# Hash attention and router: groups of four units, the mask's bits on four row quarters, first pair by tokens

## The chip, the cores and the metric

The kernel runs on one core of one Trainium2 chip. The metric is the time of one execution on the device in microseconds; of several executions the median is given. Lower is better.

## What is computed

The reference is attention with a hash mask, then a router with eight experts. B = 4 batches, 8 heads, S = 768 tokens, D = 64; the router sees N = 3072 tokens of 512 features.

```python
q_bits = (einsum('bhsd,dk->bhsk', q, proj) > 0)      # 6 bits for every query and key
k_bits = (einsum('bhsd,dk->bhsk', k, proj) > 0)
mask = bucket(q_bits)[:, :, :, None] == bucket(k_bits)[:, :, None, :]
scores = where(mask, q @ k.T / sqrt(D), -1e9)
attn = softmax(scores) @ v                            # per head
x = attn of all heads side by side                    # 3072 x 512
e = argmax(cosine(x, expert_emb) / tau); gate = softmax prob of e
out = gate * (relu(x @ w1[e]) @ w2[e])                # 512 -> 1024 -> 512
```

## The kernel before

**Tiling of the attention.** Two heads of a batch are a pair; there are 16 pairs (`pairs`), 4 to a batch. Features lie on partitions: head 0 on rows 0 to 63, head 1 on rows 64 to 127. A unit (`units`) is one block of 128 keys (c of 6) against one half of the queries (s of 2, 384 each) for both heads: 12 units in a pair, 192 in all. `scores(u)` (L553) issues for a unit two f32 matmuls, K = 64, one per head on its half of the array's rows (L560), and two bf16 matmuls that add the mask's bits into the same PSUM banks (L563): equal bits leave the score, unequal ones pull it far down. The exponential (L566, ScalarE) then writes the tile p, and VectorE adds p into `acc` (L570, L573), from which the row sums come. `attend(u)` (L579) multiplies p with the values (L585), both heads on a column half of the array each, K = 128. An f32 matmul is two passes in the trace; a bf16 matmul one.

**Order.** The loop at L720 goes over groups of G = 3 units; g counts the groups of a pair (0 to 3). In each turn it issues the scores of a group, then `attend` for the group before, and after them by hand a step of the pair's other work. `in_order` (L430) ties all instructions of an engine to this order. The steps, with g: sums of the pair before (`sums`, L596: row sums by TensorE L602, ScalarE copy, DMAs za and zc on SP) at 0; transposes of the next pair's q and k by VectorE (`prep_features`, L512) at 0 and 1; squares for the router's norm (`add_squares` ScalarE at 0, `added_squares` VectorE L424 at 1); `scale` (L612: reciprocal L615, DMA zd out, DMA rz back in broadcast) at 1, with the load of the pair three ahead (`load`, `load_values`), a piece of expert weights, the router's logits (L192) in every fourth pair, and `square` (L519: ScalarE, L524, with accumulator read) of the next pair; bits of the next pair (`prep_bits`, L529) at 2 and `store` (L629); `scaled` (L623: multiplication with rz) at 3. `run(n)` advances the placing of tokens in expert lists (`place`, VectorE), of which the last batch's share sits in pair 14, with `fill` (L323), `lists`, `places` (L338) and the first gathers by GpSimd (`fetch`, L379).

**Bits.** `prep_bits` multiplies `proj2` with the features of a pair in eight matmuls (64 rows x 32 columns, L538) into one PSUM tile, ScalarE copies it as bf16 to `hs` (L541), and eight VectorE operations (L545 for q, L549 for k) compare with 0 and write 6 and 12 rows to `qb` and `kb`, which hold 64 rows for each head.

**Buffers.** `banks()` (L448) hands out three PSUM tiles of two banks in rotation; scores, sums, bits and logits all take the next one. Six tiles p (`pts`, 2 G), two `av` banks.

**Start.** `load(0)` (L492) brings q and k of pair 0 in 128-byte pieces on the SP and ScalarE queues, 28 matmuls of ones (WARM) keep TensorE busy, GpSimd's queue brings `proj2`, VectorE transposes q and k (L517).

After the attention the experts run (L937 on), untouched by the diff.

Of the kernel before, what the change touches and what calls it, by code (L numbers as in the profile page):

```python
# [26 lines left out]
def kernel(  # L27
# [104 lines left out]
    nc.vector.scalar_tensor_tensor(out=qcon[:], in0=ksub[:], scalar=2.0 * BIT, in1=qcon[:], op0=ALU.mult, op1=ALU.add)  # L132
# [25 lines left out]
    nc.gpsimd.dma_start(gd[ZC:N, :].rearrange("(p c) o -> p (c o)", c=NC), zrow[:, 0:NC])  # L158
    nc.gpsimd.dma_start(gd[N : N + 1, :], zrow[0:1, NC : NC + 1])
    nc.gpsimd.dma_start(xd[ZC * NQ : (ZC + 1) * NQ, :].rearrange("i (f j) -> (i f) j", j=4), zrow[:, 0:4])  # L160

    proj2 = const.tile([P, 2, 32], F32, name="proj2")
    nc.vector.memset(proj2[:], 0.0)
    for h in range(2):
        nc.gpsimd.dma_start(proj2[h * D : (h + 1) * D, h, 0:HB].rearrange("d (r n) -> d r n", r=2),
                            proj.unsqueeze(1).broadcast_to([D, 2, NB]))
# [260 lines left out]
    units = [(pr, s, c) for pr in range(len(pairs)) for s in range(2) for c in range(NC)]  # L427
# [10 lines left out]
    with ExitStack() as at:  # L438
# [9 lines left out]
        def banks():  # L448
            return ps_w.tile([P, 2, 512], F32, name="banks", tag="banks")


        WARM = 28
        G = 3
# [6 lines left out]

        qbs = [ep.tile([P, 2, SH], BF16, name=f"qb{i}") for i in range(2)]
        kbs = [ep.tile([P, 2, SH], BF16, name=f"kb{i}") for i in range(2)]
        for t in qbs:
            nc.gpsimd.tensor_copy(out=t[:], in_=qcon[:, 0:1].unsqueeze(2).broadcast_to([P, 2, SH]))
        for t in kbs:
            nc.gpsimd.memset(t[:], 0.0)
# [24 lines left out]
        ld, feat, acc, av, zcs, rzs = {}, {}, {}, {}, {}, {}  # L491
        def load(pr):  # L492
            if pr >= len(pairs):
                return
            b, j = pairs[pr]
            qk = ldp.tile([P, 2, S // 32, 32], F32, name="qk", tag="qk")
            vt = ldp.tile([P, 2, NC, D], F32, name="vt", tag="vt", bufs=4)
            for g in range(NQ):
                for i, src in enumerate((q, k)):
                    (nc.scalar if pr < 2 and i else nc.sync).dma_start(  # L500
                        qk[32 * g : 32 * (g + 1), i].rearrange("t (c a) f -> t c a f", c=NC),
                        src[b, 2 * j + g // 2].rearrange("(a t c) d -> t c a d", t=32, c=NC)[
                            :, :, :, 32 * (g % 2) : 32 * (g % 2 + 1)])
            ld[pr] = (qk, vt)
# [7 lines left out]
        def prep_features(pr, i):  # L512
            if pr >= len(pairs):
                return
            t = augp.tile([P, 2, SH], F32, name="qt" if i == 0 else "kt", tag="qt" if i == 0 else "kt")
            feat[pr, i] = t
            nc.vector.transpose(t[:].rearrange("p s n -> p (s n)"), ld[pr][0][:, i].rearrange("p n f -> p (n f)"))  # L517
# [11 lines left out]
        def prep_bits(pr):  # L529
            if pr >= len(pairs):  # L530
                return
            b = (qbs[pr % 2], kbs[pr % 2])
            ps = banks()
            for i in range(2):
                for s in range(2):
                    for h in range(2):
                        r0 = 32 * (2 * i + s)
                        nc.tensor.matmul(ps[r0 : r0 + 32, h, 0:SH], lhsT=proj2[h * D : (h + 1) * D, h, :],  # L538
                                         rhs=feat[pr, i][h * D : (h + 1) * D, s, :], start=True, stop=True)
            hs = rp.tile([P, 2, SH], BF16, name="hs", tag="hs", bufs=1)  # L540
            nc.scalar.copy(out=hs[:], in_=ps[:, :, 0:SH])  # L541
            for s in range(2):
                for h in range(2):
                    r0 = 32 * s
                    nc.vector.tensor_scalar(out=b[0][h * D : h * D + NB, s], in0=hs[r0 : r0 + NB, h], scalar1=0.0,  # L545
                                            scalar2=2.0 * BIT, op0=ALU.is_gt, op1=ALU.mult)
                for h in range(2):
                    r0 = 64 + 32 * s
                    nc.vector.tensor_scalar(out=b[1][h * D : h * D + HB, s], in0=hs[r0 : r0 + HB, h], scalar1=0.0,  # L549
                                            scalar2=ksub[r0 : r0 + HB, 0:1], op0=ALU.is_gt, op1=ALU.subtract)  # L550


        def scores(u):  # L553
            pr, s, c = units[u]
            qt, kt, qb, kb = feat[pr, 0], feat[pr, 1], qbs[pr % 2], kbs[pr % 2]
            ps = banks()
            kc = slice((c % HC) * P, (c % HC + 1) * P)
            rows = [slice(h * D, (h + 1) * D) for h in range(2)]
            for h in range(2):
                nc.tensor.matmul(ps[:, h, 0:SH], lhsT=kt[rows[h], c // HC, kc], rhs=qt[rows[h], s, :],  # L560
                                 start=True, stop=False)
            for h in range(2):
                nc.tensor.matmul(ps[:, h, 0:SH], lhsT=kb[rows[h], c // HC, kc], rhs=qb[rows[h], s, :],  # L563
                                 start=False, stop=True)
            p = pts[u % NPT]
            nc.scalar.activation(p[:, :, 0:SH], ps[:, :, 0:SH], ACT.Exp, scale=ESCALE)  # L566
            if c == 1:
                a = op.tile([P, 2, SH], F32, name="acc", tag="acc", bufs=3)
                acc[pr, s] = a
                nc.vector.tensor_tensor(out=a[:], in0=pts[(u - 1) % NPT][:, :, 0:SH], in1=p[:, :, 0:SH], op=ALU.add)  # L570
            elif c > 1:
                a = acc[pr, s]
                nc.vector.tensor_tensor(out=a[:], in0=a[:], in1=p[:, :, 0:SH], op=ALU.add)  # L573
# [5 lines left out]
        def attend(u):  # L579
            pr, s, c = units[u]  # L580
# [3 lines left out]
            for h in range(2):  # L584
                nc.tensor.matmul(ps[h * D : (h + 1) * D, 0 : SH + 1], lhsT=vt[:, h, c, :], rhs=p[:, h, 0 : SH + 1],  # L585
                                 start=(c == 0), stop=(c == NC - 1))
# [118 lines left out]
        load(0)  # L705

# [3 lines left out]
        nc.sync.dma_start(emb[:], expert_emb[:, :])  # L710
        nc.sync.dma_start(tau_t[:], tau.unsqueeze(0).broadcast_to([E, 1]))
# [4 lines left out]
        for pr in range(1, 3):  # L716
            load(pr)
            load_values(pr)
        U, PU = len(units), 2 * NC
        for u0 in range(0, U + G, G):  # L720
# [3 lines left out]
            run(7 if j == 2 and end else 3)  # L724
            for u in range(u0, u0 + G):
                if u < U:
                    scores(u)
                if end and j == 2:
                    if g == 1 and u == u0 + 1:
                        begin(b, spare(2 * E * NC))  # L730
                    elif g == 2:
                        run(2 if u < u0 + 2 else 99)
                    elif g == 3 and u == u0 + 1:
                        fill(b, spare(4 * NS))
                        listed = lists(slots, src[0][:], NS, rp)
            if u0 == U:
                scaled_last(len(pairs) - 1, 0)
            for u in range(u0 - G, u0):
                if 0 <= u < U:
                    attend(u)  # L740
                if u0 == U and u == U - G:
                    scale_last(len(pairs) - 1, 1)
            if end and j == 2 and g == 3:
                places(listed, pos[0][:], NS, banks()[:, 0], rp)
                early = [fetch(pos[0], 0, 2, ZC + 1)]
            if pr == len(pairs):
                break
            if g == 0:
                if pr > 0:
                    sums(pr - 1)  # L750
                prep_features(pr + 1, 0)
                if pr > 1:
                    add_squares(pr - 2, rp)
                if pr == 2:
                    prep_experts(1)
                if j == 2 and b >= 0:
                    gates(b, rp, 0)
            elif g == 1:
                prep_features(pr + 1, 1)
                if pr > 1:  # L760
                    added_squares(pr - 2)
# [19 lines left out]
            elif g == 2:  # L781
                prep_bits(pr + 1)
                if pr > 1 and not (end and j == 2):
                    store(pr - 2)
                if j == 2 and b >= 0 and not end:
                    gates(b, rp, 2)
                if j == 3 and end:
                    bound(1)
            else:
                if pr > 0:  # L790
                    scaled(pr - 1)
                if pr == 1:
                    prep_experts(0)
# [4 lines left out]
                if j == 2 and end:  # L798
                    store(pr - 2)
                    gates(b, rp, 2)  # L800
# [3 lines left out]
                if j == 3 and end:  # L804
                    scale_last(pr, 0)
# [562 lines left out]
```

## Time and profile before

| | |
|---|---|
| median of 3 runs | 720.61 us (719.82 to 723.15) |
| profiled execution, its own time | 721.9 us |
| its span | 719.9 us |
| mean granted TensorE clock | 0.991 |
| TensorE matmul busy | 691.8 us, 96% of the span |
| VectorE busy | 479.4 us |
| ScalarE busy | 307.5 us |
| GpSimd busy | 193.9 us |

Busy times by stage, from the trace (us; the second row is the attention's steady part, the fourth the experts):

| stretch | PE | DVE | ACT | POOL |
|---|---|---|---|---|
| 0 to 9.8 | 7.97 | 5.27 | 1.49 | 9.12 |
| 9.8 to 336.2 | 320.69 | 261.77 | 221.26 | 7.59 |
| 336.2 to 360 | 21.89 | 16.87 | 11.82 | 18.45 |
| 360 to 719.9 | 341.21 | 195.49 | 72.91 | 158.77 |

How to read the profile: PE is TensorE's matmuls, PEld its weight loads, DVE VectorE, ACT ScalarE, POOL GpSimd, SP the engine that issues most DMAs. The ends of matmuls are modelled, so starts are what to compare. A form such as 64*128 after an operation is its rows * columns of the array. In the groups of instructions a row ends with the busy time, the mean of one, and the idle time of the engine ahead of it with what ended it. A wait for several things is put down to the last. A profiled execution is one run; its time lies 1.3 us above the median.

### The profile page before, as it was taken

What the parts mean: (1) busy time and instruction counts of PE and PEld (TensorE: products, weight loads), DVE (VectorE), ACT (ScalarE), POOL (GpSimd) and SP (SyncE); (2) the same over time, 40 slices, a digit from 0 to 9 for tenths busy, and PEclk for the clock granted to TensorE, in tenths of its full rate; (3) what the DMA queues carried; (4) which work ended last, traced back from release to release, by engine and by line L of the source; (5) the groups of instructions that cost most, each with busy time, mean ns of one, the idle gap of its engine ahead of it and who ended that gap; (6) DMA issues with size and microseconds to landing.
All of it is one profiled execution on the core that took longest, in us unless ns stands there. A gap on an engine that the chain in (4) does not pass through costs nothing.

```text
span 719.9 us, 11583 instructions
## 1 busy us (share of the span) xinstructions
PE 691.8 (96%) x4197; PEld 427.7 (59%) x4197; DVE 479.4 (67%) x984; ACT 307.5 (43%) x565; POOL 193.9 (27%) x202
## 2 busy tenths in 40 slices
PE   8999999999999999998899998999999999999992
PEld 6444443444434444343475666969797879797970
DVE  5867787789778897698752022798867786866100
ACT  2777765767757767665420111213222222222210
POOL 5000000000000000003714763246554647350160
PEclk9999999999999999999999999999999999999997
DMA  9733477743678645523581139335454545443320
GB/s 141 125 54 75 74 112 140 135 78 93 118 141 140 127 70 118 92 34 64 98 264 37 56 132 321 129 139 183 143 170 141 167 149 172 146 157 132 123 75 20
DMA packets 198337, 87.90 MB, mean 122 GB/s; under 512 B 171569, under 2 KB 179565, under 8 KB 198264
## 3 DMA queue, kind: packets, MB, share of 16 engines
q1 hardware_dynamic: 183704, 68.35, 40.5%
q0 software_dynamic: 6720, 13.67, 6.3%
q10 hardware_dynamic: 7840, 4.98, 2.5%
q8 instruction: 37, 0.61, 0.4%
q14 instruction: 36, 0.29, 0.2%
HBM read 82.57 MB, written 13.31 MB: 133 GB/s over the span
## 4 chain that ended last, share of the span: by engine, by line
PE 79%; DVE 7%; POOL 4%; issue 3%; DMA 3%; ACT 1%; SPq 0%; POOLq 0%; DVEq 0%; ACTq 0%
PE ps_h L1091 15%; PE banks L560 15%; PE av L585 15%; PE ps_y L984 11%; PE ps_h L1120 10%; PE ps_h L976 6%; PE banks L563 4%; POOL xg L379 3%; DVE acc L573 2%; PE banks L538 2%; PE banks L602 1%; DMA proj<-in_proj_dram 1%; DVE kt L517 1%; DMA out_dram<-y,osrc 0%; DMA qk<-in_k_dram 0%
## 5 line engine op out<-in xcount | busy, mean ns | idle before, releaser
L566 ACT ACTIVATE p<-banks 128x768 f32<-128x768 f32 x192 | 152.1, 812 | 44.8 <-PE banks L563 42.0
L560 PE MATMUL banks<-qt,kt 64*128 64x384 f32 x768 | 162.3, 500 | 0.0
L585 PE MATMUL av<-p,vt 128*64 128x385 f32 x768 | 138.5, 495 | 0.0
L573 DVE TENSOR_TENSOR acc<-acc,p 128x768 f32<-128x768 f32 x128 | 122.1, 954 | 20.7 <-ACT p L566 11.0
L379 POOL DMA_INDIRECT xg<-xd,pos x96 | 103.6, 1079 | 101.3 <-ACT ht L1095 41.1
L1066 DVE TENSOR_TENSOR tm<-ps_h,tm 128x192 f32<-128x192 f32 (+1 forms) x210 | 72.2, 368 | 56.5 <-PE ps_h L1120 30.4
L560 PEld LDWEIGHTS banks<-qt,kt 64*128 64x128 f32 x768 | 64.8, 186 | 60.9 <-issue 32.7
L984 PE MATMUL ps_y<-w,ht 128*128 128x512 f32 x224 | 98.4, 593 | 0.0
L585 PEld LDWEIGHTS av<-p,vt 128*64 128x64 f32 x768 | 49.4, 136 | 75.8 <-issue 73.8
L229 POOL TENSOR_TENSOR nrm<-l,half 128x6 f32<-128x6 f32 x4 | 5.4, 1340 | 264.6 <-DVE l L206 264.6
L984 PEld LDWEIGHTS ps_y<-w,ht 128*128 128x128 f32 x224 | 41.9, 190 | 47.4 <-issue 47.1
L563 PE MATMUL banks<-qb,kb 64*128 64x384 bf16 x384 | 63.7, 323 | 1.1 <-DVE kb L549 1.1
L1095 ACT ACTIVATE ht<-tm 128x192 f32<-128x192 f32 x96 | 32.6, 362 | 74.7 <-DVE tm L1066 74.7
L1091 PE MATMUL ps_h<-tx,xT 128*128 128x192 f32 x288 | 56.0, 332 | 2.6 <-DVE xT L1026 2.6
L991 DVE TENSOR_SCALAR y<-ps_y,gg 128x512 f32<-128x512 f32 x8 | 6.0, 751 | 70.7 <-PE ps_y L984 70.7
L1091 PEld LDWEIGHTS ps_h<-tx,xT 128*128 128x128 f32 x288 | 49.3, 194 | 2.9 <-DVE xT L1026 2.9
L995 POOL DMA_INDIRECT out_dram<-y,src x24 | 28.2, 1175 | 79.8 <-ACT y L1111 17.2
L978 ACT ACTIVATE ht<-ps_h 128x128 f32<-128x128 f32 (+1 forms) x48 | 15.0, 313 | 74.9 <-PE ps_h L976 73.3
L976 PE MATMUL ps_h<-xge,w 128*128 128x256 f32 (+1 forms) x256 | 43.2, 328 | 0.7 <-DVE xT L663 0.7
L976 PEld LDWEIGHTS ps_h<-xge,w 128*128 128x128 f32 x256 | 38.6, 191 | 5.8 <-issue 1.7
L1091 PE MATMUL ps_h<-xgt,w 128*128 128x192 f32 x192 | 39.5, 328 | 0.0
L570 DVE TENSOR_TENSOR acc<-p,p 128x768 f32<-128x768 f32 x32 | 30.5, 954 | 11.9 <-ACT p L566 11.8
(274 smaller groups left out, 845.4 us busy)
## 6 DMA issues: line engine op xcount, KB each, us to landing
w<-in_moe_w_dram SPq DMA_DIRECT2D x20, 2048.0 KB
qk<-in_q_dram SPq DMA_DIRECT2D x64, 96.0 KB
vt<-in_v_dram SPq DMA_DIRECT2D x16, 384.0 KB
xd<-xb SPq DMA_DIRECT2D x64, 96.0 KB
rz<-zd SPq DMA_DIRECT2D x30, 192.0 KB
qk<-in_k_dram SPq DMA_DIRECT2D x56, 96.0 KB
w<-in_moe_w_dram SPq DMA_DIRECT2D x8, 512.0 KB
w<-in_moe_w_dram ACTq DMA_DIRECT2D x2, 2048.0 KB
```

Source lines behind the costliest of these rows:

```text
L379: dma = nc.gpsimd.indirect_dma_start(out=xg[:, g, :], out_offset=None, in_=xd[0 : width * NQ, :], in_offset=bass.IndirectOffsetOnAxis(ap=p ...
L560: nc.tensor.matmul(ps[:, h, 0:SH], lhsT=kt[rows[h], c // HC, kc], rhs=qt[rows[h], s, :], start=True, stop=False)
L563: nc.tensor.matmul(ps[:, h, 0:SH], lhsT=kb[rows[h], c // HC, kc], rhs=qb[rows[h], s, :], start=False, stop=True)
L566: nc.scalar.activation(p[:, :, 0:SH], ps[:, :, 0:SH], ACT.Exp, scale=ESCALE)
L573: nc.vector.tensor_tensor(out=a[:], in0=a[:], in1=p[:, :, 0:SH], op=ALU.add)
L585: nc.tensor.matmul(ps[h * D : (h + 1) * D, 0 : SH + 1], lhsT=vt[:, h, c, :], rhs=p[:, h, 0 : SH + 1], start=(c == 0), stop=(c == NC - 1))
L976: nc.tensor.matmul(ph[:, 0:n], lhsT=w1s[i][:, d, f * P : (f + 1) * P], rhs=xt[:, d, 0:n], start=(d == 0), stop=(d == ND - 1))
L984: nc.tensor.matmul(py[:], lhsT=ht[:, f, j * P : (j + 1) * P], rhs=w2s[i][:, f, :], start=(f == 0), stop=(f == NF - 1))
L1066: nc.vector.tensor_tensor(out=out, in0=ps, in1=s, op=ALU.add)
L1091: nc.tensor.matmul(out, lhsT=l[:, d, f * P : (f + 1) * P], rhs=r[:, d, :], start=(d == 0), stop=(d == ND // 2 - 1))
L1095: acted[0] = nc.scalar.activation(ht[:, f + j * NF // 2, k * HT : (k + 1) * HT], c, ACT.Relu).ins
L1120: nc.tensor.matmul(out, lhsT=l[:, f, :], rhs=r[:, f, :], start=(f == 0), stop=(f == NF // 2 - 1))
```

## The change

G becomes 4, so a pair of heads has three groups (g of 0 to 2), p has eight tiles, and the steps are dealt to the groups anew. The key blocks of a pair are taken alternately from the two halves of the keys; `scores` now issues two units at once: scores of the first on their half rows, four bit matmuls of 32 rows (two heads, two key blocks, one row quarter each, into four banks), scores of the second. To that end `qb` holds the query bits on both quarters of a head, in the two orders, and `kb` one key half on each quarter; the constants ride in the compare (`qthr`, `qmul`). Pair 0 is loaded by tokens, in 256-byte pieces, turned by TensorE and copied by ScalarE (q) and VectorE (k). `proj2` comes on SP's queue, pair 1 is loaded earlier, WARM is 14.

```diff
-        WARM = 28
-        G = 3
+        WARM = 14
+        G = 4
...
-    units = [(pr, s, c) for pr in range(len(pairs)) for s in range(2) for c in range(NC)]
+    units = [(pr, s, c, c // 2 + c % 2 * HC) for pr in range(len(pairs)) for s in range(2) for c in range(NC)]
...
+            if pr == 0:
+                for i, src in enumerate((q, k)):
+                    for h in range(2):
+                        (nc.scalar if i else nc.sync).dma_start(by_token(qk, i)[:, :, h * D : (h + 1) * D],
+                                                                src[b, h].rearrange("(p c) d -> p c d", c=NC))
+                return
...
+            if pr == 0:
+                ps = banks()
+                for c in range(NC):
+                    nc.tensor.transpose(ps[:, c // HC, c % HC * P : (c % HC + 1) * P], by_token(ld[pr][0], i)[:, c, :], ident[:])
+                (nc.vector.tensor_copy if i else nc.scalar.copy)(out=t[:], in_=ps[:, :, 0:SH])
+                return
...
+            for h in range(2):
+                for i, o, n in ((0, 0, 32 + HB), (32, 0, HB), (0, 32, HB)):
+                    nc.vector.tensor_scalar(out=b[0][h * D + o : h * D + o + n, int(n == HB)], in0=hs[i : i + n, h],
+                                            scalar1=qthr[i : i + n, 0:1], scalar2=qmul[i : i + n, 0:1],
+                                            op0=ALU.is_gt, op1=ALU.mult)
+            for h in range(2):
+                n = slice(64, 64 + 32 + HB)
+                nc.vector.tensor_scalar(out=b[1][h * D : h * D + 32 + HB], in0=hs[n, h], scalar1=0.0,
+                                        scalar2=ksub[n, 0:1], op0=ALU.is_gt, op1=ALU.subtract)
...
+        def scores(u):
+            pr, s, _, c = units[u]
+            qt, kt, qb, kb = feat[pr, 0], feat[pr, 1], qbs[pr % 2], kbs[pr % 2]
+            ps = [banks() for _ in range(2)]
+            kc = slice(c * P, (c + 1) * P)
+            def score(i):
                 for h in range(2):
+                    n = slice(h * D, (h + 1) * D)
+                    nc.tensor.matmul(ps[i][:, h, 0:SH], lhsT=kt[n, i, kc], rhs=qt[n, s, :], start=(i == 0), stop=(i == 1))
+            score(0)
             for h in range(2):
+                for i in range(2):
+                    n = slice(h * D + 32 * i, h * D + 32 * (i + 1))
+                    nc.tensor.matmul(ps[i][:, h, 0:SH], lhsT=kb[n, kc], rhs=qb[n, s ^ i, :], start=(i == 1), stop=(i == 0))
+            score(1)
...
+        for h in range(2):
+            nc.sync.dma_start(proj2[h * D : (h + 1) * D, h, 0:HB].rearrange("d (r n) -> d r n", r=2),
+                              proj.unsqueeze(1).broadcast_to([D, 2, NB]))
...
+        load(1)
         load_values(0)
...
+            if g == 1 and 1 < pr < len(pairs):
+                added_squares(pr - 2)
+            run(7 if g == 1 and j == 2 and end else 4)
...
             if g == 0:
                 if pr > 0:
                     sums(pr - 1)
-                prep_features(pr + 1, 0)
+                    for i in range(2):
+                        prep_features(pr + 1, i)
...
+                if j == 2 and end:
+                    begin(b, spare(2 * E * NC))
...
             elif g == 1:
-                prep_features(pr + 1, 1)
-                if pr > 1:
-                    added_squares(pr - 2)
+                if pr == 0:
+                    for i in range(2):
+                        prep_features(pr + 1, i)
+                prep_bits(pr + 1)
                 if pr > 0:
                     scale(pr - 1)
                 load(pr + 3)
...
-            elif g == 2:
-                prep_bits(pr + 1)
-                if pr > 1 and not (end and j == 2):
-                    store(pr - 2)
...
             else:
+                if j == 2 and end:
+                    places(listed, pos[0][:], NS, banks()[:, 0], rp)
+                    early = [fetch(pos[0], 0, 2, ZC + 1)]
                 if pr > 0:
                     scaled(pr - 1)
+                if pr > 1:
+                    store(pr - 2)
```

The steps after `load(pr + 3)` in g = 1 stay where they were: logits, then `square(0)` and `square(pr + 1)`, then `gates` (L241).

## The prediction, on record before the result

> **What bounds the kernel now.** I read the head of the page and its chain first, then TensorE's table of waits, then the timeline of a few groups, last ScalarE's part of it.
>
> ```profile
> span 719.9 us, 11583 instructions
> ...
> PE 79%; DVE 7%; POOL 4%; issue 3%; DMA 3%; ACT 1%; SPq 0%; POOLq 0%; DVEq 0%; ACTq 0%
> ...
> L566 ACT ACTIVATE p<-banks 128x768 f32<-128x768 f32 x192 | 152.1, 812 | 44.8 <-PE banks L563 42.0
> ```
>
> TensorE holds 79% of the chain that ended last. ScalarE's exponentials (L566) wait for TensorE, not the other way round. The table of waits for 9 to 336 us shows that the attention stage is nearly pure matmul:
>
> ```profile
> engine line waited for: us in total, times, longest us
> PE banks L192 <- DVE ssq__163 L424: 2.5, 3, 1.0
> PE banks L338 <- DVE half__3160 L330: 1.2, 1, 1.2
> PE banks L563 <- DVE kb L549: 1.1, 1, 1.1
> PE av L323 <- DVE col L316: 0.8, 1, 0.8
> ```
>
> So what TensorE does per group of units sets the time there, and the first row (router logits waiting for a sum of squares) is the largest wait left. One group of three units, from the timeline (start, duration):
>
> ```profile
> 152.44 0.92 PE L560 MATMUL banks<-qt,kt 64*128 64x384 f32 x4
> 153.19 0.33 PE L563 MATMUL banks<-qb,kb 64*128 64x384 bf16 x2
> 153.35 0.81 PE L560 MATMUL banks<-qt,kt 64*128 64x384 f32 x4
> 153.99 0.33 PE L563 MATMUL banks<-qb,kb 64*128 64x384 bf16 x2
> 154.16 0.81 PE L560 MATMUL banks<-qt,kt 64*128 64x384 f32 x4
> 154.80 0.33 PE L563 MATMUL banks<-qb,kb 64*128 64x384 bf16 x2
> 155.06 2.16 PE L585 MATMUL av<-p,vt 128*64 128x385 f32 x12
> 157.15 0.92 PE L560 MATMUL banks<-qt,kt 64*128 64x384 f32 x4
> ```
>
> Take differences of starts; the durations contain a modelled pipeline. Scores of a unit take 153.99-153.35 = 0.64 us, its bits 153.35-153.19 = 0.16, a unit 0.805. The bits follow the scores without a gap: both rows have the form 64*128. Where the form changes there is a gap. Bits of 0.16 began at 154.80, attend (L585) only at 155.06: 0.10 late. The first unit of a group lasts 153.35-152.44 = 0.91 instead of 0.81: its weight load, pulled ahead elsewhere, lies open (0.105). Attend takes 2.09 where six passes of 0.323 make 1.94. A group is 157.15-152.44 = 4.71 us: 3 x 0.805 + 1.94 + 0.35 for two changes of form.
>
> **What the skill says.** "TensorEngine Tiling (Array Packing)", Key Properties: a change of the tiling mode drains TensorE, while tiles of one mode run independently. The trace agrees: from its exact starts, every change of form that no other engine held up (some 170) costs 0.091 to 0.099 us beyond the streaming, also where only the rows change (128*128 to 64*128: 0.092 to 0.098); 8*128 to 64*128 shows 0.125. "TensorE: Matmul & The Clock Gate", LDWEIGHTS: the load's time goes with its columns, not rows. The trace agrees: 0.105 us lie open for 128 f32 columns, 0.05 for 64, 0.026 for 32. Same page, Part 3: four K=32 matmuls on four row quarters run together (3.07 times measured there). No run here shows 32-row bf16 tiles. Same page, Part 1 on queue depths: ScalarE is a strict FIFO. In this trace too it never passes one instruction by another.
>
> **The change, part by part.**
>
> *Bits on four quarters.* 192 units become 96 pairs. Four bit matmuls of two units, if they run at once, take 0.16 instead of 2 x 0.16: -0.16 a pair. But each pair goes 64*128, 32*128, 64*128: two changes of form that are not there now. Their price: 0.093 drain twice, 0.105 for the f32 weights of the second scores, and for the bf16 weights something between 0 and the 0.105 of f32. A bf16 load of 128 columns lasts 94 ns in the trace, an f32 load of 32 columns 103, of which 0.026 lies open; I take 0.015. Pair: 2 x 0.642 + 0.162 + 2 x 0.093 + 0.105 + 0.015 = 1.752 against 1.613 now, +0.139; x 96 = **+13.3 us**. Bounds: -0.16 x 96 = -15.4 (no drain), +22 (open bf16 load), +29 (bits two by two).
>
> *Groups of four.* 64 groups become 48, each saving two changes: 16 x 0.35 = **-5.6**.
>
> *Bits moved to the second group of a pair* (`prep_bits` now in g = 1, ahead of `square` in ScalarE's order). Now the square (L524) runs while TensorE attends. These rows of ScalarE show the pieces:
>
> ```profile
> 152.61 0.80 ACT L541 CAST hs<-banks 128x768 bf16<-128x768 f32 x1
> ...
> 186.90 1.48 ACT L524 ACTIVATE qksq<-qk 128x1536 bf16<-128x1536 f32 x1
> 188.27 0.19 ACT L524 ACTIVATION_READ_ACCUMULATOR qksq<-qk 128x1 f32 x1
> ```
>
> After: the copy hs waits for L538, which comes after attend, and the square, then the first exponential of the next group, queue behind it. Let e be the end of L538's streaming (152.34 here). hs starts at e + 0.27 and takes 0.80; the square with its read 1.56; exp 0.81; from an exp's end to TensorE's start 0.06 (at 15.85 us TensorE waits for such an exp). So the first bank is free at e + 3.52. Three PSUM tiles go round, a group now takes four, so its fourth (the second of its second pair) is the first's. Its first writer is that pair's bits, ready at e + 0.09 + 0.105 + 0.642 + (0.093 + 0.015 + 0.162) + (0.093 + 0.105 + 0.642) + 0.642 + 0.093 = e + 2.68. TensorE stands for 0.84 us, and all behind it: it is in order. Groups of three never met this. Over the pairs: 8 x 0.84; pair 0 with two squares 2.4; three with the logits' copy between, about 0.5 each; three with the small exponential of `gates` (0.23) as well, 1.1 each: **+13.9**. Elsewhere in a group the tile is freed at 2.3 against 2.6 us: a slack of some 0.3, no stall.
>
> *Sum of squares moved to the start of g = 1.* It now precedes that group's sums in VectorE's queue, so the logits at the group's end find it done: L192's wait goes, 2.5 in the table, 3.0 by starts, **-3.0**.
>
> *Start.* Pair 0 comes in 256-byte pieces, half as many packets; it lands at 8.8 now. The first packets move at 2.1. Between no gain and half of the 6 us of moving, I take 2.5 us earlier: 6.3. proj now rides SP behind q; today it lands at 10.8 just in time, and nothing suggests that it is later than k then. Then 6 transposes each (0.11 a piece, L200's spacing), copies of 0.80 and 0.95, L538 at +2.6, hs to +4.25. `scores` now needs all eight bit operations, 8 x 0.31, before its first bits: 13.2, against 13.56 now. With two stalls of 0.34 gone there: -0.8. In pair 0 `prep_features(1)` stands in g = 1 right before `prep_bits(1)`: its two transposes (0.97 each) queue behind three sums that end some 5.5 us into the group, TensorE arrives at 6.4: about +1.0. A halved clock, after WARM is cut and TensorE waits 2.9 us for the bits: 0 to 2, I take 0.5. v of pair 0, now behind pair 1's load in SP's queue, lands near 15 (load of pair 1: 5.4 us after 6.3, then 1.5 plus issue), wanted near 20: hidden. emb and tau are wanted in pair 1. **+0.7** (from -2 to +4).
>
> *VectorE and SP.* Bits: eight operations of 0.31 for four of 0.255 and four of 0.31, +0.2 a pair; VectorE is busy 262 of 326 us, hidden. `scaled` and `store` come one group nearer to `scale`: in the trace the reciprocal (172.2) is some 7 us ahead of rz landing, and only 4 to 5 us of VectorE's work remain between. It idles about 2 us a pair, of the 4 that it has. If that cover is gone TensorE waits for sums through the p buffers. I take **+0.5**, up to +6. SP sends the same DMAs in the same order; its round from reciprocal to reciprocal, 21 us, fits into the longer pair (21.9).
>
> *Last batch's placing* moves to one group. By VectorE's queue in pair 14 (9.5 us of sums, 5.2 of placing, 2.5 of bits, 2 of transposes), `places` waits some 2 us, as L338 and L323 do now (2.0): **0**. The gather starts about 1 us into pair 15, as now; its 20 us end with that pair. Experts: untouched.
>
> Sum: 13.3 - 5.6 + 13.9 - 3.0 + 0.7 + 0.5 = +19.8. The profiled execution took 721.9 us (span 719.9), 1.3 over the median of 720.61; on the median: **740.4 us**.
>
> **Rivals.** (a) *Drains are paid, but the late exponentials are hidden* (the square is scheduled elsewhere or the tile is released earlier than I read): -13.9, 726.5. For: the square's wait is not in the trace of before. Against: queue order and ring size are in the code. (b) *The change from 64 to 32 rows doesn't drain*: the pair costs 1.446, the stage's matmuls fall by 15.4 + 5.6 + a little lead = 21.8; TensorE then meets the late bank earlier (e + 2.28), the stalls become 19.8. Sum -3.8: 716.8, faster; without the late bank, 697. For: 32-row tiles aren't shown, and both row forms use all columns. Against: 128 to 64 rows drains. It decides as soon as a change costs under 0.03 us in all. (c) *The four bit matmuls run two by two*, or one weight load of each lies open: +15.4, 756. Against: L538's eight tiles run at once, 0.35 us for 0.32.
>
> **How the numbers follow.** Main 0.60, (a) 0.16, (b) 0.12, of which a third without the late bank, (c) 0.12. The main case's own range is 732 to 749 (start, VectorE, bf16 load). To leave out no more than 0.2 the range takes in (a) and the cheaper part of (c): 722 to 752. A measurement of this kernel tells about 0.5% (3.6 us) from nothing. Faster by more: most of (b), 0.10; within: the rest of it and the low tail of (a), 0.07; slower 0.83.
>
> **What would show it.** Right: 0.09 gaps on both sides of the 32-row bits, pairs of 1.75 us, a wait of TensorE's 32-row bits for ScalarE's exp of 0.8 us once a pair of heads, L524 now directly before that exp; no L192 row in the waits. Wrong: bits that follow the scores without a gap; bit matmuls 0.16 apart; VectorE ending most of TensorE's waits; first bits far from 13 us.

## The result and the profile after

The changed kernel takes 754.5 us (median of 4 runs, 751.2 to 756.3), the kernel before 721.9 beside it: ratio 1.045, 95% interval 1.039 to 1.050. The forecast was 740.4, range 722 to 752, that is 19.8 us more; 32.6 came. The sign and most of the mechanism held, the size didn't. The profiled execution took 754.7 us, span 752.9.

The page of the changed kernel, its head, its chain by engine and four groups:

```profile
span 752.9 us, 11534 instructions
...
PE 57%; DVE 16%; DMA 15%; issue 4%; SPq 3%; ACT 2%; POOL 1%; ACTq 0%; POOLq 0%; DVEq 0%
...
L591 ACT ACTIVATE p<-banks 128x768 f32<-128x768 f32 x192 | 149.1, 811 | 38.5 <-PE banks L586 31.2
...
L651 DVE TENSOR_TENSOR xT<-xT,rz 128x768 f32<-128x768 f32 x15 | 14.4, 958 | 56.5 <-DMA rz<-zd 56.5
...
L586 PEld LDWEIGHTS <-kb 32*128 32x128 bf16 x384 | 11.4, 91 | 65.7 <-issue 59.5
...
L586 PE MATMUL banks<-qb,kb 32*128 32x384 bf16 x384 | 39.4, 333 | 8.2 <-ACT p L591 5.3
```

The chain used to be 79% TensorE; now it is 57%, and VectorE and DMA stand in it with 16% and 15%. The L651 row names the pair of them: VectorE stood 56.5 us in front of 15 multiplications by rz (`scaled`), waiting for the DMA that brings rz. The table of TensorE's waits, 0 to 400 us (total, times, longest):

```profile
PE banks L586 <- ACT p L591: 5.3, 14, 1.7
PE banks L334 <- DVE half__3170 L326: 4.6, 1, 4.6
PE banks L685 <- DVE zl L677: 3.2, 1, 3.2
PE banks L586 <- DVE kb L566: 2.9, 1, 2.9
PE av L610 <- ACT xT L616: 1.7, 2, 0.9
```

L192's wait for the sum of squares is gone. In its place stand 32-row bits that wait for ScalarE's exp (14 times, 15 were forecast), the last batch's `places` (L334), the last reciprocal zl, and a wait that no step of the prediction had: attend for ScalarE's xT.

Where in time it lies: experts begin at 393.40 instead of 359.99 us, +33.4; after that both take the same (359.5 and 359.9). Measured from one pair's row sums to the next pair's, a pair of heads takes 21.58 instead of 20.45 us in the first pairs, and pair 14 takes 30.62 instead of 23.66.

A plain pair of units and the late exponential, TensorE's timeline of the changed kernel (start, duration):

```profile
49.32 0.92 PE L580 MATMUL banks<-qt,kt 64*128 64x384 f32 x4
50.16 0.34 PE L586 MATMUL banks<-qb,kb 32*128 32x384 bf16 x4
50.44 1.56 PE L580 MATMUL banks<-qt,kt 64*128 64x384 f32 x8
51.93 0.33 PE L586 MATMUL banks<-qb,kb 32*128 32x384 bf16 x1
52.52 0.34 PE L586 MATMUL banks<-qb,kb 32*128 32x384 bf16 x3 [0.26 <-ACT p L591]
52.79 0.92 PE L580 MATMUL banks<-qt,kt 64*128 64x384 f32 x4
```

From bits to bits 51.93 - 50.16 = 1.77 us: a pair of units (1.764 by exact starts), forecast 1.752, two units before 1.613. Ahead of the bits the exact starts show 0.095 us beyond the streaming (at 94 of the 96 pairs; at the other two TensorE waits or its clock is halved), behind them 0.100 (at 95 of 96): 64 to 32 rows drains. Where nothing holds them, the four bit matmuls start within 11 ns, so they do run together. At 51.93 one of the four goes, its three companions follow at 52.52: they wait for a PSUM tile that the exp has not yet read.

### The profile page after: what moved, and what is told of

Same layout as the page of the kernel before. It is cut to its first block, busy times and chain, and to the rows that moved or that the text cites. A ratio compares the mean times of both kernels' runs of the same rounds, so it can differ in the third digit from the quotient of the medians.

```text
span 752.9 us, 11534 instructions
## 1 busy us (share of the span) xinstructions
PE 710.2 (94%) x4181; PEld 420.2 (56%) x4181; DVE 488.7 (65%) x986; ACT 305.0 (41%) x566; POOL 192.5 (26%) x200
## 4 chain that ended last, share of the span: by engine, by line
PE 57%; DVE 16%; DMA 15%; issue 4%; SPq 3%; ACT 2%; POOL 1%; ACTq 0%; POOLq 0%; DVEq 0%
PE ps_h L1119 15%; PE ps_y L1012 10%; PE ps_h L1148 9%; PE av L610 7%; PE banks L580 6%; PE ps_h L1004 6%; DMA zd<-zc 5%; DMA rz<-zd 4%; DVE qb L561 3%; DVE acc L598 2%; DMA qk<-in_k_dram 2%; SPq L512 1%; DVE acc L595 1%; PE banks L586 1%; PE banks L555 1%
## 5 line engine op out<-in xcount | busy, mean ns | idle before, releaser
L591 ACT ACTIVATE p<-banks 128x768 f32<-128x768 f32 x192 | 149.1, 811 | 38.5 <-PE banks L586 31.2
L1094 DVE TENSOR_TENSOR tm<-ps_h,tm 128x192 f32<-128x192 f32 (+1 forms) x210 | 72.2, 367 | 56.5 <-PE ps_h L1148 30.8
L610 PEld LDWEIGHTS av<-p,vt 128*64 128x64 f32 x768 | 51.1, 138 | 79.9 <-issue 75.6
L580 PEld LDWEIGHTS banks<-qt,kt 64*128 64x128 f32 x768 | 62.7, 187 | 52.3 <-issue 28.5
L1123 ACT ACTIVATE ht<-tm 128x192 f32<-128x192 f32 x96 | 32.6, 362 | 74.4 <-DVE tm L1094 74.4
L651 DVE TENSOR_TENSOR xT<-xT,rz 128x768 f32<-128x768 f32 x15 | 14.4, 958 | 56.5 <-DMA rz<-zd 56.5
L586 PEld LDWEIGHTS <-kb 32*128 32x128 bf16 x384 | 11.4, 91 | 65.7 <-issue 59.5
L586 PE MATMUL banks<-qb,kb 32*128 32x384 bf16 x384 | 39.4, 333 | 8.2 <-ACT p L591 5.3
```

Of the source, the lines that this page charges most:

```text
L580: nc.tensor.matmul(ps[i][:, h, 0:SH], lhsT=kt[n, i, kc], rhs=qt[n, s, :], start=(i == 0), stop=(i == 1))
L586: nc.tensor.matmul(ps[i][:, h, 0:SH], lhsT=kb[n, kc], rhs=qb[n, s ^ i, :], start=(i == 1), stop=(i == 0))
L591: nc.scalar.activation(p[:, :, 0:SH], ps[i][:, :, 0:SH], ACT.Exp, scale=ESCALE)
L1094: nc.vector.tensor_tensor(out=out, in0=ps, in1=s, op=ALU.add)
L1123: acted[0] = nc.scalar.activation(ht[:, f + j * NF // 2, k * HT : (k + 1) * HT], c, ACT.Relu).ins
```

## The experiments

They ran on three chips, each time beside the kernel before: e1, e2, e3 and e7 beside 721.2 us, e4b, e5b, e10 and e11 beside 720.5, and e4, e5, e8 and e9 on a chip on which it took 767.0 (below: the disturbed chip). The changed kernel itself was measured once, beside 721.9. A difference across the first two groups and the changed kernel is uncertain by 1 to 1.5 us on that account; the third group is compared within itself only.

**e7: what a change of form costs by itself.** Kernel before, bits on the 32 rows that hold them:

```diff
+            few = [slice(h * D, h * D + 32) for h in range(2)]
...
-                nc.tensor.matmul(ps[:, h, 0:SH], lhsT=kb[rows[h], c // HC, kc], rhs=qb[rows[h], s, :],
+                nc.tensor.matmul(ps[:, h, 0:SH], lhsT=kb[few[h], c // HC, kc], rhs=qb[few[h], s, :],
```

> The kernel before with one edit: its two bit matmuls of a unit take only the 32 rows of a head that hold the bits, so their form is 32*128 instead of 64*128; everything else, the group of three and the number of matmuls, as before. This counts the cost of a change of form by itself. Theory 1: in a group three changes into the bits (0.094 drain and about 0.015) and two out of them (0.101 and 0.105 of open weight load) come on top: 0.74 us, 64 groups, 47 us: about 768. Rival (no drain between 64 and 32 rows; what the changed kernel shows comes from four tiles at once): 721.

Measured: 761.6 us against 721.2 (ratio 1.055, 1.048 to 1.063), +40. A group of three, TensorE's timeline:

```profile
159.24 0.92 PE L561 MATMUL banks<-qt,kt 64*128 64x384 f32 x4
160.09 0.34 PE L564 MATMUL banks<-qb,kb 32*128 32x384 bf16 x2
160.35 0.92 PE L561 MATMUL banks<-qt,kt 64*128 64x384 f32 x4
...
162.58 2.16 PE L586 MATMUL av<-p,vt 128*64 128x385 f32 x12
```

Scores to attend is 162.58 - 159.24 = 3.34 us instead of 2.62: +0.72 where 0.74 was expected, 46 us over 64 groups. That the whole moved by 40 fits with slower groups covering waits: the three waits of L192 are gone from e7's trace, and pair 14, which waits most, grew by 0.7 us only, against 2.9 for the first pairs. The rival without a drain falls.

**e3: the changed kernel with 64-row bits** (old layout and compares back, the rest as changed; of its edit, the matmuls):

```diff
...
             for i in range(2):
+                ps.append(banks())
+                for h in range(2):
+                    nc.tensor.matmul(ps[i][:, h, 0:SH], lhsT=kt[rows[h], i, kc], rhs=qt[rows[h], s, :],
+                                     start=True, stop=False)
+                for h in range(2):
+                    nc.tensor.matmul(ps[i][:, h, 0:SH], lhsT=kb[rows[h], i, kc], rhs=qb[rows[h], s, :],
+                                     start=False, stop=True)
...
```

> The changed kernel with the bits as before the change: per unit two bf16 matmuls of 64 rows, the old layout of qb and kb and the old compares; groups of four, order and start as changed. Theory 1: the changes of form inside a pair go, 96 x 0.151 = 14.5 us, while the rotating PSUM tile is wanted 0.1 us earlier (1.6 us more of waiting): about 741.5. Rival (the drains are hidden or made up elsewhere, the loss lies in the schedule alone): within 3 us of 754.5.

Measured: 741.4 us, 13.1 less, where 13 was expected. The waits for exp grew from 5.3 to 9.9 us in the table, 4.6 where 1.6 was expected; why the total hits the forecast all the same is open. So of the change's parts the bits on four row quarters cost 13 us net, and some 20 us remain with the other stalls unmended.

**e1: the square ahead of the bits' copy.**

```diff
             elif g == 1:
+                if pr == 0:
+                    square(0)
+                square(pr + 1)
...
-                if pr == 0:
-                    square(0)
-                square(pr + 1)
```

> The changed kernel with one step moved: in the second group of a pair the square of the next pair (L541) stands ahead of the bits' copy in ScalarE's order, as it did before the change. Theory 1 (late exponentials cost TensorE 0.58 us a pair and 2.1 in pair 0, 10.9 us in all, since 52.52 against 51.94 in the trace): TensorE's waits of L586 for exponentials go, the time falls by 8 to 11 us, to about 745. Rival (the pair's length is set by VectorE and the round from reciprocal to rz, so TensorE only waits elsewhere): less than 3 us.

Measured: 749.2 us, 5.3 less, where 8 to 11 were expected. The mechanism is right, but half of its gain was lost elsewhere. TensorE's waits in this kernel:

```profile
PE banks L334 <- DVE half__3170 L326: 5.3, 1, 5.3
...
PE av L319 <- DVE col L312: 2.4, 2, 1.2
...
PE banks L555 <- DVE qt L534: 1.6, 1, 1.6
...
PE banks L586 <- ACT p L591: 0.6, 2, 0.4
```

The exponentials' row fell from 5.3 to 0.6, and first pairs take 20.99 us instead of 21.58: 0.59 each, what the timeline showed. Then VectorE is late: L334, L319 and L555 wait for it, rows that were 4.6, 0.9 and 0.4. They have grown by 3.4 us together, more than half of what is missing.

**e2: scaled one group later.**

```diff
+            if g == 0 and 1 < pr < len(pairs):
+                scaled(pr - 2)
...
-                if pr > 0:
+                if pr == len(pairs) - 1:
                     scaled(pr - 1)
```

> The changed kernel with the multiplication by rz (scaled) moved from the third group of a pair to the start of the first group of the next (in the last pair it stays). Theory 1: VectorE's 56.5 us of idle ahead of that multiplication delay all behind it in its queue (next transposes, placing, the last reciprocals), and that costs TensorE 10 to 12 us (late second half of L555, 4.6 at places, 3.2 at the last zl and the halved clock after both): time falls to 742 to 745. Rival 1 (VectorE is not the bottleneck and its idle costs nothing; the stalls of the last batch come from dealing the placing to one group): within 2 us of 754.5. Rival 2: the reading of rz is only moved and TensorE waits for the sum of squares instead: a row L188 <- DVE ssq of 3 us or more, gain under 6.

Measured: 745.5 us, 9.0 less. VectorE's first row now reads

```profile
DVE xT L651 <- DMA rz<-zd: 34.7, 15, 4.0
```

instead of 56.5. `places` waits 1.9 instead of 4.6, pair 14 takes 27.21 us instead of 30.62. Neither rival fits: the idle did cost, and no row for the sum of squares appeared. The gain is 1 to 3 us short of what I gave it, and 34.7 us of the idle are still there.

**e4, e4b: both moves** (the two diffs above).

> The changed kernel with both moves: the square ahead of the bits' copy and scaled at the start of the next pair. Apart they gave 5.3 and 9.0 us; in the trace of the first TensorE's waits for exponentials were gone (10 us) but others for VectorE had grown. Theory 1 (the rest of the square's gain was eaten by VectorE standing late behind rz): together more than the sum, 18 to 20 us, about 735. Rival (VectorE is full, whatever it waits for): the sum or less, 740 to 742.

This was on the disturbed chip (the kernel before 767 us, 761 to 776). In the trace of e4 ScalarE waited 13.4 us, in three waits during the last pairs, for something that is none of the core's engines; 779.4 us, ratio 1.016, tells nothing on the theories. Again on another chip:

> The same kernel as before with both moves (square first, scaled later), again: the first time it ran on a chip on which the kernel before took 767 us and where, in the last pairs, ScalarE stood 13 us for something that is no engine of the core. Theory 1 as before: 18 to 20 us under the changed kernel, ratio to the kernel before about 1.02. Rival: the sum of the two apart or less, 1.026 or more.

Measured: 738.2 us, ratio 1.023 (1.020 to 1.027), 16.3 under the changed kernel. That lies between the sum of the two (14.3) and my 18 to 20, and the interval holds the rival's 1.026: it doesn't decide whether the two gains only add. By the traces the experts begin 14.2 us earlier than in the changed kernel (4.4 in e1, 9.9 in e2), but here TensorE's clock is halved from 13.8 to 20.6 us, which the changed kernel's trace doesn't have and which costs about 3 us. First pairs 20.99.

**e5, e5b: and the bits on 64 rows.**

> The last one with the bits on 64 rows as well: groups of four, order mended in two places, no form change inside a pair. Theory 1: the 14.5 us of form changes come off, no late exponential can eat part of them: 735 - 14.5 = 720.5, level with the kernel before; left over are the start and the last batch (some 11 us) against 5.6 of saved group changes and 3.0 of the logits' wait. Rival (VectorE becomes the bound as TensorE gets faster): above 725.

On the disturbed chip: 768.6 against 767.0, ratio 1.0025 (0.9994 to 1.0056). Again:

> The kernel with both moves and 64-row bits, again for the same reason. Theory 1: 14.5 us under the last one, ratio to the kernel before 1.00. On the disturbed chip the two stood 10.8 us apart with 5 us of foreign waits in one and more in the other. Rival (VectorE is the bound now): 1.007 or more.

Measured: 725.1 us, ratio 1.007 (1.004 to 1.010). The bits give 13.1 us here too, so the form changes are worth 13 with and without the late exponentials. But the rest is still 4.6 us behind the kernel before, as the rival had it, although a first pair takes 20.09 us against 20.45. Pair 14 takes 27.1 against 23.7, and pairs 1 to 13 together 278.0 against 277.0. In these pairs (36 to 315 us) TensorE waits 5.8 us:

```profile
PE banks L576 <- ACT p L584: 3.2, 4, 1.0
PE av L603 <- ACT xT L609: 1.7, 2, 0.9
PE av L316 <- DVE col L309: 0.9, 1, 0.9
```

Only the last row names VectorE, so it isn't simply the bound. But the four late exponentials of the first row stand in ScalarE's queue right behind the square of `add_squares`, and ScalarE's own table has

```profile
ACT xsq L410 <- DVE xT L644: 5.5, 5, 1.5
```

L644 is the multiplication by rz. What is left of the wait for rz (37.3 us of VectorE's idle in this trace) thus reaches TensorE by way of ScalarE.

**e8: k of pair 1 on SP's queue** (on e5; one word: `nc.sync` for all of `load(1)`).

> The last one with the keys of pair 1 loaded on SP's queue instead of ScalarE's. In the changed kernel ScalarE issues those four loads until 9.52 us and only then, at 9.57, copies q of pair 0 that TensorE had turned by about 8.2. Theory 1: the copy starts some 1.2 us earlier and with it the first bits: 1 to 1.5 us less. Rival: SP's longer queue delays values and later loads, no gain or a loss of up to 1 us.

On the disturbed chip: 769.4 us, ratio 1.0018 (0.999 to 1.0045). In its trace the bits' first matmul comes 1.2 us earlier than in e5 (8.73 instead of 9.95), but the first bits only 0.46: then VectorE's copy of k, done at 9.49, is last. No gain that can be told.

**e9: two more moves** (on e8: the last reciprocal first, and the placing of batches 0 and 1 begun a group later).

> The last one with two more moves: scale_last of the last pair's first half stands ahead of scaled and store in its group, so its reciprocal does not queue behind rz; and the placing of batches 0 and 1 begins at the end of a pair's third group, not of its second. Theory 1: the first takes 2.4 us of wait of L685 and about 2 us of halved clock after it away; the second tells whether attend's two waits of 1.04 us for ScalarE's xT copy come from begin writing into a finished av bank: 4 to 6.5 us less in all, about 713. Rival for the second: the waits come from the group that spans two halves and stay.

On the disturbed chip: 778.6 us, ratio 1.015 (1.009 to 1.022): worse than e8. Its trace is of the slowest of the six executions (786.7 us). TensorE's table:

```profile
PE av L316 <- DVE col L309: 14.6, 2, 7.7
```

Begun later, the placing isn't done when `fill` wants it, twice 7 us. But attend's two waits of 1.04 us for xT, at the same place in every other variant, are not in this trace: they come from `begin` writing into a finished av bank in the second group. Why the dependency then names the xT copy is open.

**e11: e8 with only the last reciprocal first.**

```diff
+                if j == 3 and end:
+                    scale_last(pr, 0)
                 if pr == len(pairs) - 1:
                     scaled(pr - 1)
...
                     bound(1)
-                    scale_last(pr, 0)
```

> The last one with k of pair 1 loaded on SP's queue and scale_last of the last pair's first half ahead of scaled and store in its group; the placing begins where it does in the changed kernel (begun later it cost two waits of 7 us at fill). Theory 1: first bits 1.2 us earlier, L685's wait of 2.4 us and 2 us of halved clock after it gone: 4 to 5.5 us under the last one, ratio 0.993 to 0.995. Rival (the end waits for the gathers by GpSimd, which take 20 us from the places on): only the start's 1.2 us.

Measured: 726.2 us, ratio 1.007 (1.005 to 1.009): no gain over e5b. Yet the experts begin at 364.06 instead of 368.63 us, 4.6 earlier, as expected, so the gathers of the rival didn't hold them (no row of TensorE's waits names GpSimd). Stretches of its trace show where that went (us, PE busy, PEld, DVE, ACT, POOL, granted clock, DMA share, GB/s):

```profile
361.70:364.00 2.30, 1.55 (x12) 1.15 (x12) 0.58 (x2) 0.00 (x0) 0.00 (x0) 0.52 0.98 151
364.00:368.50 4.50, 4.44 (x11) 3.54 (x12) 2.41 (x4) 0.38 (x1) 0.00 (x0) 0.50 0.29 47
368.50:373.00 4.50, 4.50 (x37) 2.86 (x36) 0.00 (x0) 0.86 (x2) 0.00 (x0) 0.99 0.98 301
...
457.30:460.70 3.40, 3.40 (x13) 3.40 (x12) 2.92 (x6) 0.36 (x1) 2.79 (x3) 0.51 0.99 328
```

A wait of 2.6 us for the other half's zl now stands at the very end, and TensorE does the next 6.8 us at half its clock. e5b has 6.8 us of it too, but ahead of the experts; here 4.5 us lie in them, 2.3 us of work lost. The other 1.7 us are lost in the stretch at 457 us, which e5b's trace doesn't have. The experts' code is the same in all runs, yet such a stretch stands, 90 to 93 us into the experts, in some traces (before, changed, e2, e11) and not in others (e1, e3, e4b, e5b, e7, e10), so some 2 us of a profiled execution are chance.

**e10: one term alone, in the kernel before.**

```diff
+            if g == 1 and 1 < pr < len(pairs):
+                added_squares(pr - 2)
             run(7 if j == 2 and end else 3)
...
                 prep_features(pr + 1, 1)
-                if pr > 1:
-                    added_squares(pr - 2)
```

> The kernel before with one line moved: the sum of squares stands at the start of the second group, ahead of that group's sums and k's transpose, as in the changed kernel. It measures one term of the prediction by itself. Theory 1: the three waits of L192 (0.91, 0.91 and 1.20 us by starts) go: 3.0 us less, ratio 0.996. Rival (SP's round, in which the reciprocal waits for zc, sets the length of these pairs): no change.

Measured: 719.4 us, ratio 0.9992 (0.9976 to 1.0008). In its trace L192 has no wait, and the experts begin at 356.96 us, 3.03 earlier: the term is exactly what was forecast. Of the total 1.1 us is left by the medians and 0.6 by the ratio, and the interval includes a ratio of 1. No version that I ran beats the kernel before beyond doubt.

## Why the prediction was wrong

By its own terms (us, forecast against what the runs showed; the rows overlap in part and need not add to 32.6):

| term | forecast | shown |
|---|---|---|
| bits on quarters, two changes of form | +13.3 | +14.5 by starts (96 x 0.151); 13.1 when undone (e3; e5b against e4b) |
| groups of four | -5.6 (0.35 a pair) | not run alone; a first pair without the rest 20.09 against 20.45, -0.36 |
| late exponentials | +13.9 | about 11 by starts; 5.3 (e1) to 7.3 (e4b against e2) net when undone |
| sum of squares first | -3.0 | -3.0 in the stage (e10); in the total not told from nothing |
| start | +0.7 | first bits 1.45 us later instead of 0.4 earlier |
| VectorE and SP | +0.5 | at least +9.0 (e2, which takes 22 of the 56.5 us of idle away) |
| placing in one group | 0 | part of VectorE's; with it, pair 14 +7.0 |
| attend's wait for xT | none | +2.1, from `begin` in the second group (e9) |
| half clock after waits | 0.5, in the start | +3.4 ahead of the experts, none in the start |

**The step that failed is "VectorE and SP".** It saw the right place: `scaled` one group nearer to `scale`, VectorE idle for rz. It took 7 us from the reciprocal to rz and 4 to 5 us of work between, called the idle 2 us a pair and priced it at 0.5, with 6 as the end. The 7 us were too short already in the trace that it read. In the kernel before, at the reciprocal that the step names, VectorE had finished its work and still waited for rz, 8.9 us after the reciprocal's start:

```profile
172.19 0.22 DVE L615 RECIPROCAL zc<-zc 128x12 f32<-128x12 f32 x1
...
181.13 0.96 DVE L626 TENSOR_TENSOR xT<-xT,rz 128x768 f32<-128x768 f32 x1 [0.15 <-DMA rz<-zd]
```

Over the whole attention of the kernel before that wait was small, because other work covered the round:

```profile
DVE xT L626 <- DMA rz<-zd: 1.4, 3, 0.7
```

VectorE's timeline of the changed kernel:

```profile
53.35 0.23 DVE L640 RECIPROCAL zc<-zc 128x12 f32<-128x12 f32 x1
53.49 4.08 DVE L598 TENSOR_TENSOR acc<-acc,p 128x768 f32<-128x768 f32 x4
61.75 0.96 DVE L651 TENSOR_TENSOR xT<-xT,rz 128x768 f32<-128x768 f32 x1 [4.18 <-DMA rz<-zd]
```

The round is 61.75 - 53.35 = 8.4 us, the work between 4.1, the idle 4.2. Over 15 pairs it is 3.8 on average: all of the slack that the step itself allowed VectorE ("of the 4 that it has"). With the slack gone, later items of its queue are late, and what was priced at nothing in other steps falls due: next transposes late for L555, `places` (forecast: about 2 us, as before; 4.6 by the table), the last reciprocal (3.2). With the multiplication moved back by a group (e2) these rows become nothing, 1.9 and 2.4.

**What no step had at these places: the clock.** After the waits for `places` (4.6 us) and for the last zl (3.2 us) TensorE of the changed kernel runs at half speed for 3.4 us each time (columns as in e11's table):

```profile
358.60:362.00 3.40, 3.40 (x16) 1.63 (x18) 1.43 (x5) 1.13 (x2) 1.44 (x2) 0.50 0.39 108
385.90:389.30 3.40, 3.40 (x16) 1.22 (x12) 3.16 (x6) 0.00 (x0) 1.89 (x2) 0.50 0.79 112
```

That is 1.7 us of work lost each time, on top of the waits. Only the start was thought of, at 0.5; there this trace shows 1.00, and e4b's, with the same start, 0.50 for 6.8 us.

**Right in kind, off in size.** The late exponential: ScalarE's timeline shows why 0.84 became 0.58.

```profile
49.49 0.80 ACT L558 CAST hs<-banks 128x768 bf16<-128x768 f32 x1 [2.79 <-PE banks L555]
50.19 1.49 ACT L541 ACTIVATE qksq<-qk 128x1536 bf16<-128x1536 f32 x1
51.57 0.19 ACT L541 ACTIVATION_READ_ACCUMULATOR qksq<-qk 128x1 f32 x1
51.67 2.90 ACT L591 ACTIVATE p<-banks 128x768 f32<-128x768 f32 x4
```

The square starts 0.70 after the copy that lasts 0.80, four exps of 0.81 take 2.90: queued instructions overlap by about 0.1 us, and I had added durations (which add to 3.50, not 3.52). That a mended stall gives back half (e1) is the other lesson: TensorE then ran into VectorE.

The start: L555 begins at 10.42, not at 8.9.

```profile
7.39 1.50 PE L531 MATMUL banks<-ident,qk 128*128 128x128 f32 x12
...
9.57 0.80 ACT L532 COPY qt<-banks 128x768 f32<-128x768 f32 x1 [6.56 <-DMA qk<-in_k_dram]
...
10.42 0.53 PE L555 MATMUL banks<-qt,proj 64*32 64x384 f32 x4 [1.53 <-ACT qt L532]
```

The transposes begin at 7.39, where 6.3 was taken; then ScalarE's copy of q stands behind ScalarE's own loads of pair 1, issued until 9.53, which the step did not count. And the eight compares took 3.0 us, not 2.5. The 1.0 us forecast for pair 1's transposes did not come: TensorE waits 0.15 us there.

Rival (a) had the exponentials hidden: they were not. (b), no drain, is refuted by the 96 gaps and e7. (c), two by two, ends near the measured time (756) by luck: the four start within 11 ns.

What stays open: with form, square and part of rz's wait mended, pair 14 still takes 3.5 us more than before (e5b), and how much of that is the placing dealt to one group was not separated from what is left of rz's wait (37.3 us of idle in e5b). Groups of four and the new start were not run alone.

## What to carry to other kernels

Count the changes of form that an edit adds before counting the matmuls that it saves: here 0.16 us saved stood against 0.3 us of drains and open weight loads. When a consumer moves nearer to its producer, write down the whole round trip (here reciprocal, write, read back: 8.4 us) and the queued work that covers it; if the idle comes near the engine's slack, price everything behind it in that queue, and in the queues that wait for it, not the idle. A mended wait is worth only what the next engine leaves over: the same square gave 5.3 us in e1 where about 11 stood in the starts. And look at the clock after any wait of some us.

## What was not expected of the hardware

- 64-row and 32-row tiles drain into each other like any other change of form: 0.095 us in (94 of 96 times), 0.100 out (95 of 96).
- Four 32-row bf16 matmuls into four banks start within 11 ns and take little more than the 0.16 us of streaming of one; their weight loads last 91 ns, and some 0.02 us of them lies open in a pair of 1.764 us.
- In the changed kernel's trace, after waits of 4.6 and 3.2 us, TensorE's granted clock was 0.50 for 3.4 us; in e5b and e11, at waits of 2.9 and 2.6 us, for 6.8 us. The wait of 2.9 us before the first bits left it at 1.00 in the changed kernel; at the same wait in e4b it was 0.50 for 6.8 us.
- Back-to-back ScalarE instructions overlapped by about 0.1 us: 0.69 to 0.71 us from exp to exp of 0.81.
